# Seven products of quarters for three pairs of blocks in the second product of a transformer block

## The chip, the cores and the metric

The kernel runs on one core of one Trainium2 chip. Its time is device time in microseconds (us), from one launch. A core has TensorE (PE in the profile, its weight loads PEld), VectorE (DVE), ScalarE (ACT), GpSimd (POOL) and SyncE (SP, here a queue that issues transfers). Each takes its instructions in the order in which they are written, and semaphores hold one back until others are done.

## The reference

One block with 2048 tokens of width 512: local dilated attention, then a dense layer with a squared ReLU. The change lies in the last quarter of the dense layer.

```python
def _B_ref(x, w1, b1, w2, b2):          # x 2048x512, w1 512x1792, w2 1792x512
    h = jnp.einsum("bsd,df->bsf", x, w1) + b1
    r = jnp.where(h > zero, h, zero)
    h = r * r
    out = jnp.einsum("bsf,fd->bsd", h, w2) + b2
    return out

h = x + _A_ref(_layernorm(x, axis=-1), A_wqkv, A_wo)
h2 = h + _B_ref(_layernorm(h, axis=-1), B_w1, B_b1, B_w2, B_b2)
```

## The kernel before

Every float32 operand of a product is held as a high part (a cast, `hi`) and a low part (the difference, `lo`), and each product is three products of parts: high by high, low by high, high by low.

The tokens are worked on in four passages `u` of 512 tokens, four tiles of 128 each. The 1792 hidden units are 14 blocks `f` of 128. In a passage the *first product* (w1) makes a block of hidden values in a PSUM bank, ScalarE and VectorE turn it into the squared ReLU in two parts, and the *second product* (`mlp2`, w2) adds that block into four banks `acc`, one per tile: 12 matmuls of 512 columns (4 tiles, 3 terms). The high parts of w2 stay in `big_h`; the low parts of 12 blocks are stashed in DRAM (`w2l_d`), and some of them at a time lie in `big_l`, whence `fetch` brings the next when a place comes free. `big_l` also holds the transposed tokens.

In the last passage (`u` = 3) the first product goes by pairs of blocks (`PAIRS`, seven of them), each as seven products of quarters (Winograd's form of Strassen's scheme): a quarter has 256 features or 128 units or 256 tokens, so that each of the 7 products is 6 matmuls of 256 columns in place of 8 x 6 for the whole. It needs sums of quarters of the tokens (made once: `s32`, `a_h`, `a_l`) and of the weights, made for each pair: `t_load` brings the raw w1 columns (`traw`), `t_sums` makes four differences in place (on VectorE for pairs 0 and 1, on GpSimd after), `t_split` makes the parts `th` and `tl`. `products_a` does four products (24 matmuls) into the four banks `b` of the tuple `XB`, and copies two of them to `p`; `products_b` does the other three (18 matmuls), two of them on top of the first ones, and adds up. `second`, `squared` and `rest` make ReLU, square and parts of the pair's two blocks f and g (`r`, `rh`, `rl`).

No scheduler moves anything: an engine's order is the order of the code. `at(k, fn, ...)` puts a call off to the end of the k-th slot from now (`due`), and `end_slot` runs the calls of the current slot, so their place in an engine's order is the place of that `end_slot`. A step n of the last passage has two slots: `products_a(n)`, one second product; `products_b(n)`, another second product (from step 2 on). The raw weights of pair n + 2 are loaded at the start of step n, their sums made in its second slot, and their parts in the first slot of step n + 1. At the end, two blocks' second products go tile by tile, each tile followed by `finish` (the residual is added, the tile goes out), and `last_tile` does the last tile in two halves of 256 columns. Three things of earlier passages reach into this one: the residual `h` of the last tiles gets b2 on GpSimd (`add_b2`, L694), goes to DRAM (`spill`, L697), and comes back (`unspill`).

## Time and profile before

| | before |
|---|---|
| median of 3 runs (lowest to highest) | 501.11 us (500.86 to 548.89) |
| the profiled execution | 500.91 us |
| its span, first to last instruction | 499.1 us |
| TensorE busy, matmuls | 494.2 us (99%), 2411 |
| VectorE, ScalarE, GpSimd busy | 383.7, 305.7, 354.6 us |
| granted TensorE clock, mean | 1.000 of full speed |

The rows further down are of the profiled execution, in us from the start of its span. The time between the execution and its span, 500.91 - 499.1, lies around the kernel. In the rows of an engine a number in square brackets is its idle time before that instruction, with what ended it. Matmuls overlap, so the pace of a group is read from the chain, where each piece ends as the next begins.

### The profile page before, as it was taken

The numbers are of one execution on the slowest core, as the hardware profiler recorded it, in microseconds if no ns is written. First come the engines' busy times: TensorE is split into PE (matmuls) and PEld (weight loads), VectorE is DVE, ScalarE is ACT, GpSimd is POOL, SyncE is SP. The second block draws the span as 40 slices with busy tenths as digits, with TensorE's granted clock in tenths as the row PEclk, the third lists the DMA queues.
The fourth block names the chain that finished last, engine by engine and source line by source line (L and its number), as shares of the span: only waits on it lengthen the run. The fifth ranks groups of instructions, "written<-read, shape, count | busy, mean of one in ns | idle before, by whom it ended". The sixth has DMA issues, their size and how long they took to land.

```text
span 499.1 us, 7514 instructions
## 1 busy us (share of the span) xinstructions
PE 494.2 (99%) x2411; PEld 420.6 (84%) x2411; DVE 383.7 (77%) x526; ACT 305.7 (61%) x543; POOL 354.6 (71%) x429
## 2 busy tenths in 40 slices
PE   8999999999999999999999999999999999999997
PEld 7998888888888888888888888888888888998986
DVE  6479899999989989998979989897984257733233
ACT  4634778668346757478564556866454968766551
POOL 5714798996775999888878777787889353885610
PEclk9999999999999999999999999999999999999999
DMA  8779979889788899689776945977680575355212
GB/s 269 201 215 244 281 253 297 272 268 310 209 219 260 294 286 259 185 226 248 219 253 210 218 143 164 269 236 258 201 202 14 130 193 163 117 158 169 64 42 87
DMA packets 113584, 103.67 MB, mean 208 GB/s; under 512 B 33672, under 2 KB 82056, under 8 KB 113544
## 3 DMA queue, kind: packets, MB, share of 16 engines
q1 hardware_dynamic: 112600, 102.66, 70.1%
q10 hardware_dynamic: 944, 0.52, 0.3%
q8 instruction: 19, 0.31, 0.3%
q14 instruction: 21, 0.17, 0.1%
HBM read 72.65 MB, written 24.25 MB: 194 GB/s over the span
## 4 chain that ended last, share of the span: by engine, by line
PE 98%; DMA 1%; ACT 0%; ACTq 0%; DVE 0%; issue 0%
PE mm L231 49%; PE acc L924 30%; PE wo L231 9%; PE mm L837 7%; PE tr L204 2%; DMA wraw<-in_A_wqkv_dram 1%; PE half L947 0%; ACTq L570 0%; ACT big_h L152 0%; ACT xh L152 0%; DVE h L949 0%
## 5 line engine op out<-in xcount | busy, mean ns | idle before, releaser
L414 POOL TENSOR_TENSOR pr<-pr 128x512 f32<-128x512 f32 (+1 forms) x128 | 134.1, 1048 | 35.6 <-DVE pr L357 30.2
L231 PE MATMUL mm<-big_l,w_h 128*128 128x512 f32 x336 | 88.5, 390 | 0.0
L357 DVE TENSOR_TENSOR pr<-ex,v 128x1024 f32<-128x1024 f32 x62 | 75.6, 1221 | 12.0 <-POOL o L414 9.2
L344 DVE TENSOR_TENSOR pr<-qp,k 128x1024 f32<-128x1024 f32 x64 | 76.8, 1200 | 6.1 <-ACT qp L271 3.3
L380 DVE TENSOR_REDUCE ex<-pr 128x64 f32<-128x1024 f32 x64 | 78.4, 1225 | 1.8
L231 PEld LDWEIGHTS mm<-big_l,w_h 128*128 128x128 f32 x336 | 63.0, 188 | 13.4 <-ACT r L894 0.3
L155 POOL TENSOR_TENSOR rl<-r,rh 128x512 fp32r<-128x512 f32 x42 | 54.9, 1306 | 24.2 <-ACT rh L152 20.1
L231 PE MATMUL mm<-big_l,xh 128*128 128x512 f32 (+1 forms) x208 | 56.3, 379 | 0.0
L231 PE MATMUL mm<-big_h,xh 128*128 128x512 f32 (+1 forms) x208 | 53.1, 377 | 0.3 <-ACT xh L152 0.3
L231 PE MATMUL mm<-big_h,xl 128*128 128x512 f32 (+1 forms) x208 | 52.6, 374 | 0.0
L924 PE MATMUL acc<-big_h,rh 128*128 128x512 f32 x190 | 52.1, 391 | 0.0
L924 PE MATMUL acc<-big_l,rh 128*128 128x512 f32 x190 | 52.0, 390 | 0.0
L924 PE MATMUL acc<-big_h,rl 128*128 128x512 f32 x190 | 51.7, 390 | 0.0
L231 PE MATMUL mm<-big_l,w_l 128*128 128x512 f32 x168 | 44.9, 389 | 0.0
L231 PEld LDWEIGHTS mm<-big_h,xl 128*128 128x128 f32 x208 | 38.3, 188 | 6.0
L231 PEld LDWEIGHTS mm<-big_h,xh 128*128 128x128 f32 x208 | 37.9, 188 | 6.1 <-ACT xh L152 0.5
L924 PEld LDWEIGHTS acc<-big_h,rl 128*128 128x128 f32 x190 | 35.7, 188 | 7.4
L924 PEld LDWEIGHTS acc<-big_l,rh 128*128 128x128 f32 x190 | 35.6, 188 | 7.4
L231 PEld LDWEIGHTS mm<-big_l,xh 128*128 128x128 f32 x208 | 37.4, 188 | 4.9
L924 PEld LDWEIGHTS acc<-big_h,rh 128*128 128x128 f32 x190 | 35.1, 188 | 7.1 <-DVE h L932 0.3
L894 ACT ACTIVATE r<-mm,b_sb 128x512 f32<-128x512 f32 x42 | 28.7, 684 | 16.2 <-PE mm L231 15.7
L231 PEld LDWEIGHTS mm<-big_l,w_l 128*128 128x128 f32 x168 | 31.5, 188 | 6.6
(167 smaller groups left out, 919.4 us busy)
## 6 DMA issues: line engine op xcount, KB each, us to landing
k<-qkv_d SPq DMA_DIRECT2D x50, 288.0 KB, 3.2
v<-qkv_d SPq DMA_DIRECT2D x46, 288.0 KB, 3.2
qkv_d<-y SPq DMA_DIRECT2D x18, 512.0 KB, 4.0
big_l<-w2l_d SPq DMA_DIRECT2D x24, 256.0 KB, 3.1
xt<-in_A_x_dram SPq DMA_DIRECT2D x16, 256.0 KB, 4.2
q<-qkv_d SPq DMA_DIRECT2D x32, 128.0 KB, 3.6
h<-in_A_x_dram SPq DMA_DIRECT2D x16, 256.0 KB, 3.3
h_d<-h SPq DMA_DIRECT2D x16, 256.0 KB, 3.4
```

The lines of the kernel that those rows point to most:

```text
L155: eng.tensor_tensor(out=dst, in0=src, in1=h, op=ALU.subtract)
L204: nc.tensor.transpose(tr[:, k, :], src[:, k * P:(k + 1) * P], ident)
L231: nc.tensor.matmul(ps, l(k), r(k), start=(n == 0), stop=(n == 3 * KB - 1))
L344: nc.vector.tensor_tensor(out=pr.rearrange("p i w h d -> p i w (h d)"), in0=qps["now"][:, j % 2].unsqueeze(2).to_broadcast([P, RI, W, GC]) ...
L357: nc.vector.tensor_tensor(out=p2, in1=vwin, op=ALU.mult, in0=e1[:, :, :, j * GH:(j + 1) * GH].unsqueeze(4).to_broadcast([P, RI, W, GH, DH]))
L380: nc.vector.tensor_reduce(out=lf[:, :, :, j * GH:(j + 1) * GH], in_=pr, axis=X, op=ALU.add)
L414: nc.gpsimd.tensor_tensor(out=dst, in0=p2[:, :, :w], in1=p2[:, :, w:2 * w], op=ALU.add)
L837: nc.tensor.matmul(ps, sta[y][:, k], mov[x][:, k], start=(first and q == 0), stop=(last and q == len(terms) - 1), skip_group_check=True)
L894: nc.scalar.activation(r, ps, AF.Relu, bias=b1_sb[:, f:f + 1])
L924: nc.tensor.matmul(acc[j], l[:, j * P:(j + 1) * P], w[f], start=(first and n < len(js)), stop=(last and n >= len(terms) - len(js)))
```

## The change

The second product of the last three pairs, (0, 7), (1, 8) and (4, 11), is done by seven products of quarters as well. The four quarters of a product are now: 256 of the 512 tokens by one of the pair's two blocks for the hidden values, and one of the two blocks by 256 of the 512 output columns for w2. Each of the seven (`part`) is 6 matmuls of 256 columns, three terms by two tiles. What this needs: `v_load` brings the raw rows of w2 for a pair, `v_sums` makes four differences on GpSimd, `v_split` the parts; `s_sums` makes four sums of the pair's hidden quarters on VectorE (`x`), `s_split` their parts. Products 1, 5, 6 and 7 add up over the three pairs in the four banks `XB` (`outer`), 4, 3 and 2 go right into `acc` (`inner`, and the loop at the end); five sums (`v`, `u2`, `u3`, `s12`, `s22`) and eight half additions to `h` put them together. `last_tile` is gone; the last product of the last tile has a bank of its own (`z`).

The second product of the other eight blocks is as before, but `PLAN` gives each step one, after `products_a`; two are left for the end of the last step.

The hidden parts of the last passage are written into the columns of `w1_h` and `w1_l` that belong to their block and are no longer needed. The raw w1 columns are two tiles under the tags of the attention's k and v. `AHEAD` is a table of the steps' first and second slots: `t_load`, `t_sums` and `t_split` move a slot or a step forward, from pair 2 on; half of each `tl` now comes from VectorE (before: from pair 3 on, both halves from GpSimd). The four unspills come together after the last step.

```diff
+WN = 3
+PLAN = {n: (1, 0) for n in range(1, 7)}
+VS = {2: 0, 3: 1, 4: 2}
+VP = ()
 HOLD = 1.0
 XS = 6
...
     def t_load(n):
         f = PAIRS[n][0]
-        tw[n] = t_tile(n, "traw")
+        tw[n] = [att.tile([P, RI, 2, P], F32, name="traw", tag="kv"[n % 2]) for _ in range(2)]
         for k in range(KB):
-            nc.sync.dma_start(tw[n][:, k], bass.AP(
...
-        b11, b12, b21, b22 = [tw[n][:, 2 * k:2 * k + 2, c] for k in (0, 1) for c in (0, 1)]
+        b11, b12, b21, b22 = [t[:, :, c] for t in tw[n] for c in (0, 1)]
         tt, sub = (nc.vector if n < 2 else nc.gpsimd).tensor_tensor, ALU.subtract
         tt(out=b11, in0=b12, in1=b11, op=sub)
...
     def t_split(n):
-        h, l = t_tile(n, "th", F32R), t_tile(n, "tl", F32R)
-        hi(h, tw[n])
-        for k, eng in ((2, nc.vector if n < 3 else nc.gpsimd), (0, nc.gpsimd)):
-            lo(eng, l[:, k:k + 2], tw[n][:, k:k + 2], h[:, k:k + 2])
+        h, l = t_tile("th", "pr"), t_tile("tl", "o")
+        raw = tw[n]
+        for k in (1, 0):
+            hi(h[:, 2 * k:2 * k + 2], raw[k])
+        for k, eng in ((1, nc.vector), (0, nc.vector if n == 2 else nc.gpsimd)):
+            lo(eng, l[:, 2 * k:2 * k + 2], raw[k], h[:, 2 * k:2 * k + 2])
         tw[n] = h, l
...
         nc.scalar.activation(rf[:, :HD], b[1], AF.Relu, bias=b1_sb[:, f:f + 1])
         tt(out=u[:, HD:], in0=b[2], in1=p[:, :HD], op=ALU.add)
...
         nc.scalar.activation(r, r, AF.Square)
-        hi(rh, r)
-        lo(nc.vector, rl, r, rh)
-        hid[R - 1, f] = rh, rl
+        if f in PAIRS[-1]:
+            at(0, parted, f, r)
+        else:
+            parted(f, r)
+    def parted(f, r):
+        rh, rl = [w[:, :, f * P:(f + 1) * P] for w in (w1_h, w1_l)]
+        n = RI if f in WINO[:WN] else R
+        src = r.rearrange("p (j c) -> p j c", j=R)[:, :n]
+        hi(rh[:, :n], src)
+        lo(nc.vector, rl[:, :n], src, rh[:, :n])
...
+    PLAIN = len(PAIRS) - WN
+    WINO = [p[i] for i in range(2) for p in PAIRS[PLAIN:]]
+    whole, vw = {}, {}
+    def v_load(q):
+        vw[q] = row("vraw"), row("vraw")
+        for r, f in zip(vw[q], PAIRS[PLAIN + q]):
+            nc.sync.dma_start(r, w2[f * P:(f + 1) * P, :])
+    def v_sums(q):
+        (b11, b12), (b21, b22) = [(r[:, :HD], r[:, HD:]) for r in vw[q]]
+        tt, sub = (nc.vector if q in VP else nc.gpsimd).tensor_tensor, ALU.subtract
+        tt(out=b11, in0=b12, in1=b11, op=sub)
+        tt(out=b12, in0=b22, in1=b12, op=sub)
+        tt(out=b22, in0=b22, in1=b11, op=sub)
+        tt(out=b21, in0=b21, in1=b22, op=sub)
+    def v_split(q):
+        if q == 0:
+            t = [work.tile([P, D], F32R, name="rh", bufs=LAG + 1) for _ in range(4)]
+        else:
+            t = [a[:, i] for a in [att.tile([P, 2, D], F32R, name="vs", tag=tag, bufs=3)
+                                   for tag in ("pr", "o")] for i in range(2)]
+        raw = vw[q]
+        vw[q] = t[:2], t[2:]
+        for i in range(2):
+            hi(t[i], raw[i])
+            at(int(q < 2), lo, nc.gpsimd, t[2 + i], raw[i], t[i])
+    def s_sums(n):
+        rf, rg = whole.pop(n)
+        (a11, a21), (a12, a22) = [(r[:, :HD], r[:, HD:]) for r in (rf, rg)]
+        x = whole[n] = row("x"), row("x")
+        tt, sub = nc.vector.tensor_tensor, ALU.subtract
+        tt(out=x[0][:, :HD], in0=a21, in1=a22, op=ALU.add)
+        tt(out=x[1][:, :HD], in0=a11, in1=a21, op=sub)
+        tt(out=x[0][:, HD:], in0=x[0][:, :HD], in1=a11, op=sub)
+        tt(out=x[1][:, HD:], in0=a12, in1=x[0][:, HD:], op=sub)
+    def s_split(n):
+        for x, f in zip(whole.pop(n), PAIRS[n - PLAIN]):
+            src = x.rearrange("p (j c) -> p j c", j=R)
+            h, l = [w[:, :, f * P:(f + 1) * P] for w in (w1_h, w1_l)]
+            hi(h, src)
+            lo(nc.vector, l, src, h)
+    def part(n, m, ps, js, first=False, last=False):
+        q, (f, g) = n - PLAIN, PAIRS[n]
+        c, d = PAIRS[q]
+        col, i0 = {1: (f, 0), 2: (g, 0), 4: (g, 2), 5: (c, 0), 6: (c, 2), 7: (d, 0), 3: (d, 2)}[m]
+        sta = [w[:, :, col * P:(col + 1) * P] for w in (w1_h, w1_l)]
+        lo_, hi_ = slice(0, HD), slice(HD, D)
+        if m < 4:
+            w, cs = f if m == 1 else g, hi_ if m == 3 else lo_
+            mov = w2_h[w][:, cs], w2_l[w][:, cs]
+        else:
+            i, cs = {5: (0, lo_), 7: (0, hi_), 4: (1, lo_), 6: (1, hi_)}[m]
+            mov = [t[i][:, cs] for t in vw[q]]
+        terms = [(x, y, j) for x, y in ((0, 0), (1, 0), (0, 1)) for j in js]
+        for k, (x, y, j) in enumerate(terms):
+            nc.tensor.matmul(ps[j], sta[x][:, i0 + j], mov[y], start=first and k == 0,
+                             stop=last and k >= len(terms) - len(js), skip_group_check=True)
     def hidden(u, f, ps, wait=0):
...
+        at(wait, lo, nc.gpsimd, rl, r, rh)
+        hid[u, f] = [lambda j, a=a: a[:, j * P:(j + 1) * P] for a in (rh, rl)]
     def hidden_now():
...
+            nc.tensor.matmul(acc[j], l(j), w[f],
                              start=(first and n < len(js)),
...
+                             (15, at, 0, t_load, 2),
...
-    fs = [f for pair_ in PAIRS for f in pair_]
-    need = [f for f in fs if f < 12 and f not in place]
+    fs = [f for pair_ in PAIRS[:PLAIN] for f in pair_]
+    need = [f for f in fs + WINO if f < 12 and f not in place]
...
-    def second_product(last=False):
-        q = used[0]
-        f = fs[q]
-        if last:
-            mlp2(u, f, acc, js[:-1])
-            mlp2(u, f, acc, js[-1:], False, True)
-        else:
-            mlp2(u, f, acc, js, q == 0)
-        used[0] += 1
+    def refill(f):
         if f < 12 and need:
             free.append(place.pop(f))
             at(1, fetch, need.pop(0))
+    def second_product():
+        q = used[0]
+        mlp2(u, fs[q], acc, js, q == 0, q == len(fs) - 1)
+        used[0] += 1
+        refill(fs[q])
+    AHEAD = {"0a": ((t_split, 1),), "0b": ((t_load, 3), (t_sums, 2)),
+             "1a": ((t_split, 2), (t_sums, 3)), "1b": ((t_load, 4), (t_split, 3), (t_sums, 4)),
+             "2b": ((t_load, 5), (t_split, 4), (t_sums, 5)),
+             "3b": ((t_load, 6), (t_split, 5), (t_sums, 6)), "4b": ((v_sums, 0), (t_split, 6), (v_sums, 1)), "5b": ((v_sums, 2),)}
+    def ahead(step):
+        for fn, m in AHEAD.get(step, ()):
+            if fn is t_load:
+                fn(m)
+            else:
+                at(0, fn, m)
     for n in range(len(PAIRS)):
-        if n + 2 < len(PAIRS):
-            t_load(n + 2)
+        if n in VS:
+            v_load(VS[n])
         products_a(n)
         if not n:
-            at(0, t_split, 1)
+            ahead("0a")
             lo(nc.vector, a_l[4], s32[4], a_h[4])
         if n:
             at(0, second, n - 1)
-            if n + 1 < len(PAIRS):
-                at(0, t_split, n + 1)
-            second_product()
-        if n in (4, 5):
-            for i in range(2):
-                at(0, unspill, R * u + 2 * (n - 4) + i)
+            ahead(f"{n}a")
+            if n - 3 in VS and not VS[n - 3]:
+                at(0, v_split, 0)
+            if n == len(PAIRS) - 1:
+                at(0, s_split, n - 2)
+                at(0, v_split, 1)
+            for _ in range(PLAN[n][0]):
+                second_product()
         end_slot(5.6)
         products_b(n)
-        if n + 2 < len(PAIRS):
-            at(0, t_sums, n + 2)
-        if n > 1:
+        ahead(f"{n}b")
+        if n > PLAIN:
+            at(0, s_sums, n - 1)
+        for _ in range(PLAN[n][1] if n else 0):
             second_product()
         if n == len(PAIRS) - 1:
             at(0, second, n)
-            second_product(True)
+            at(0, s_sums, n)
+            at(0, s_split, n - 1)
+            at(0, at, 0, s_split, n)
+            at(0, at, 0, v_split, 2)
+            for i in js:
+                at(1, unspill, R * u + i)
+            while used[0] < len(fs):
+                second_product()
         end_slot(4.9)
-    h = hs[S // P - 1]
-    for j in js[:-1]:
-        for f in fs[-2:]:
-            mlp2(u, f, acc, [j], False, f == fs[-1])
-            if j == 0:
-                end_slot(0.65)
-        at(0, finish, R * u + j, acc[j])
-        if j == 1:
-            at(0, nc.vector.tensor_tensor, h, acc[-1], h, ALU.add)
-        if j:
-            run(due)
-    last_tile(S // P - 1, fs[-2:])
+    two = {m: psum.tile([P, D], F32, name="part", tag=tag) for m, tag in zip((1, 5, 6, 7), XB)}
+    halves = {m: [t[:, j * HD:(j + 1) * HD] for j in range(RI)] for m, t in two.items()}
+    both, left, right = range(RI), slice(0, HD), slice(HD, D)
+    head, end = PLAIN, len(PAIRS) - 1
+    def outer(n):
+        for m in (1, 6, 5, 7) if n < end else (1, 6, 7, 5):
+            part(n, m, halves[m], both, n == head, n == end)
+        refill(PAIRS[n][0])
+        run(due)
+        now["slot"] += 1
+    def inner(n, m):
+        part(n, m, [acc[RI + j][:, left] for j in both], both, False, n == end)
+    for n in range(head, end):
+        outer(n)
+    inner(head, 4)
+    outer(end)
+    tt = nc.vector.tensor_tensor
+    v, u2, u3, s12, s22 = [row("c") for _ in range(5)]
+    nc.scalar.copy(v, two[1])
+    tt(out=u2, in0=two[6], in1=v, op=ALU.add)
+    tt(out=u3, in0=two[7], in1=u2, op=ALU.add)
+    tt(out=s22, in0=two[5], in1=u3, op=ALU.add)
+    tt(out=s12, in0=two[5], in1=u2, op=ALU.add)
+    for eng, i, cs, src in ((nc.gpsimd, 0, left, v), (nc.gpsimd, 1, left, v),
+                            (nc.gpsimd, 2, left, u3), (nc.gpsimd, 3, left, u3),
+                            (nc.vector, 2, right, s22), (nc.vector, 3, right, s22),
+                            (nc.gpsimd, 0, right, s12), (nc.gpsimd, 1, right, s12)):
+        h = hs[R * u + i][:, cs]
+        eng.tensor_tensor(out=h, in0=h, in1=src[:, i % RI * HD:(i % RI + 1) * HD], op=ALU.add)
+    for n in range(head + 1, end + 1):
+        inner(n, 4)
+    for i in (2, 3):
+        finish(R * u + i, acc[i])
+    z = psum.tile([P, D], F32, name="part", tag=XB[0])[:, left]
+    for m, j, ps in ((3, 0, acc[0][:, right]), (2, 0, acc[0][:, left]),
+                     (3, 1, acc[1][:, right]), (2, 1, z)):
+        for n in range(head, end + 1):
+            part(n, m, [ps, ps], [j], ps is z and n == head, n == end)
+        if m == 2 and not j:
+            finish(R * u, acc[0])
+    h = hs.pop(R * u + 1)
+    b, e = divmod(u, 2)
+    tt(out=h, in0=acc[1], in1=h, op=ALU.add)
+    nc.scalar.dma_start(out_v[b, e, 1, :, right], h[:, right])
+    tt(out=h[:, left], in0=z, in1=h[:, left], op=ALU.add)
+    nc.sync.dma_start(out_v[b, e, 1, :, left], h[:, left])
```

TensorE at the end of the last step, from the last product of `products_b` of pair 6 on (`mm`: bank of a first product, `acc`: bank of a tile, `big_h`: high parts of w2, `big_l`: low parts; `rh`, `rl` or `w_h`, `w_l`: the hidden parts). Before:

```order
L837 MATMUL mm<-wo_l,w_h 128x256 x2
L924 MATMUL acc<-big_h,rh 128x512 x4
L924 MATMUL acc<-big_l,rh 128x512 x4
L924 MATMUL acc<-big_h,rl 128x512 x4
L924 MATMUL acc<-big_h,rh 128x512 x3
L924 MATMUL acc<-big_l,rh 128x512 x3
L924 MATMUL acc<-big_h,rl 128x512 x3
```

TensorE at the same place now (`part`: one of the four banks of the new products; `rh` here: parts of the w2 sums):

```order
L843 MATMUL mm<-wo_l,w_h 128x256 x2
L1006 MATMUL acc<-big_h,w_h 128x512 x4
L1006 MATMUL acc<-big_l,w_h 128x512 x4
L1006 MATMUL acc<-big_h,w_l 128x512 x4
L1006 MATMUL acc<-w_x,w_h 128x512 x8
L1006 MATMUL acc<-w_x,w_l 128x512 x4
L970 MATMUL part<-big_h,w_h 128x256 x2
L970 MATMUL part<-big_h,w_l 128x256 x2
L970 MATMUL part<-big_l,w_h 128x256 x2
L970 MATMUL part<-rh,w_h 128x256 x2
```

Two whole second products stand behind the last step, and then the new products of 256 columns, where blocks of the last pairs went tile by tile.

GpSimd in steps 1 and 2, from the bias of tile 14 on (`h`: residual, `traw_4642`: raw columns of pair 2, `traw_4734`: of pair 3, `r`: the sum of L869). Before:

```order
L694 TENSOR_TENSOR h_4278<-h_4278,b2_sb_81 128x512
L155 TENSOR_TENSOR tl_4791<-traw_4642,th_4790 128x512
L694 TENSOR_TENSOR h_4341<-h_4341,b2_sb_81 128x512
L869 TENSOR_TENSOR r_4816<-u_4744,p_4743 128x256
L805 TENSOR_TENSOR traw_4734<-traw_4734 128x2x128
```

GpSimd at the same place now (`traw_4719`, `traw_4720`: pair 3; `traw_4829`: pair 4; L877 is what L869 was):

```order
L698 TENSOR_TENSOR h_4278<-h_4278,b2_sb_81 128x512
L809 TENSOR_TENSOR traw_4719<-traw_4719 128x2x128
L810 TENSOR_TENSOR traw_4719<-traw_4720,traw_4719 128x2x128
L811 TENSOR_TENSOR traw_4720<-traw_4720,traw_4719 128x2x128
L812 TENSOR_TENSOR traw_4720<-traw_4720 128x2x128
L698 TENSOR_TENSOR h_4341<-h_4341,b2_sb_81 128x512
L877 TENSOR_TENSOR r_4823<-u_4748,p_4747 128x256
L159 TENSOR_TENSOR tl_4841<-traw_4719,th_4840 128x512
L809 TENSOR_TENSOR traw_4829<-traw_4829 128x2x128
```

The four differences of pair 3 stand ahead of the second bias addition and of the sum of L877.

ScalarE from `products_b` of step 2 into step 3 (`th_4889`: pair 3; `r_4912` and `r_4913`: the two blocks of pair 2; `p_4951`: the copies of step 3's banks). Before:

```order
L152 CAST th_4889<-traw_4734 128x1024
L866 ACTIVATE r_4912<-mm_4838,b1_sb_83 128x256
L873 ACTIVATE r_4912<-r_4912,b1_sb_83 128x256
L884 ACTIVATE r_4912<-r_4912 128x512
L152 CAST rh_4933<-r_4912 128x512
L850 COPY p_4951<-mm_4947 128x256
L856 COPY p_4951<-mm_4950 128x256
L879 ACTIVATE r_4913<-r_4913,b1_sb_83 128x512
```

ScalarE at the same place now (`th_4939`: pair 4; `r_4921`, `r_4922`: pair 2; `p_4957`: step 3's copies):

```order
L874 ACTIVATE r_4921<-mm_4854,b1_sb_83 128x256
L881 ACTIVATE r_4921<-r_4921,b1_sb_83 128x256
L891 ACTIVATE r_4921<-r_4921 128x512
L156 CAST w1_h_88<-r_4921 128x4x128
L156 CAST th_4939<-traw_4830 128x512
L156 CAST th_4939<-traw_4829 128x512
L856 COPY p_4957<-mm_4953 128x256
L862 COPY p_4957<-mm_4956 128x256
L887 ACTIVATE r_4922<-r_4922,b1_sb_83 128x512
```

The cast of the weights' sums, now in halves and for one pair further on, stands ahead of the two copies of the next step's banks.

## Rows read from the trace of the kernel before

**Rows 1.** The page, part 1: busy us (share of the span) and instructions.

```profile
PE 494.2 (99%) x2411; PEld 420.6 (84%) x2411; DVE 383.7 (77%) x526; ACT 305.7 (61%) x543; POOL 354.6 (71%) x429
```

**Rows 2.** The chain that ended last, merged: start, us, engine, line, count.

```profile
422.05 7.92 PE mm L837 x66
429.96 2.97 PE acc L924 x12
...
445.61 2.87 PE mm L837 x24
448.49 2.75 PE acc L924 x12
...
482.79 2.15 PE mm L837 x18
484.94 9.55 PE acc L924 x42
494.49 1.44 PE half L947 x12
...
495.96 0.42 DVE h L949
```

**Rows 3.** Waits from 400 us on, by total: us, times, longest.

```profile
PEld acc L924 <- DVE h L932: 0.3, 1, 0.3
```

**Rows 4.** ScalarE's timeline in steps 3 and 4: start, us, line, operation.

```profile
450.24 1.05 ACT L152 CAST th<-traw 128x1024 fp32r<-128x1024 f32 x1
451.98 0.47 ACT L866 ACTIVATE r<-mm,b_sb 128x256 f32<-128x256 f32 x1 [0.69 <-PE mm L837]
453.62 0.51 ACT L873 ACTIVATE r<-r,b_sb 128x256 f32<-128x256 f32 x1 [1.16 <-DVE r L868]
454.16 0.63 ACT L884 ACTIVATE r<-r 128x512 f32<-128x512 f32 x1
454.82 0.62 ACT L152 CAST rh<-r 128x512 fp32r<-128x512 f32 x1
456.88 0.37 ACT L850 COPY p<-mm 128x256 f32<-128x256 f32 x1 [1.44 <-PE mm L837]
...
458.59 0.73 ACT L879 ACTIVATE r<-r,b_sb 128x512 f32<-128x512 f32 x1
```

**Rows 5.** GpSimd's timeline, steps 0 to 3: L869, sums, bias, lows.

```profile
428.11 0.74 POOL L869 TENSOR_TENSOR r<-u,p 128x256 f32<-128x256 f32 x1
428.81 0.75 POOL L805 TENSOR_TENSOR traw<-traw 128x256 f32<-128x256 f32 x1
...
432.48 1.75 POOL L694 TENSOR_TENSOR h<-h,b_sb 128x512 f32<-128x512 f32 x1
...
435.90 1.29 POOL L694 TENSOR_TENSOR h<-h,b_sb 128x512 f32<-128x512 f32 x1
...
447.01 0.74 POOL L805 TENSOR_TENSOR traw<-traw 128x256 f32<-128x256 f32 x1
...
449.47 0.74 POOL L808 TENSOR_TENSOR traw<-traw 128x256 f32<-128x256 f32 x1
451.37 2.55 POOL L155 TENSOR_TENSOR tl<-traw,th 128x512 fp32r<-128x512 f32 x2 [1.16 <-ACT th L152]
```

**Rows 6.** SyncE's issues in step 2: the spill of tile 15, raw columns.

```profile
437.30 0.54 SPq L697 DMA_DIRECT2D h_d<-h  x1
...
438.42 2.51 SPq L798 DMA_DIRECT2D traw<-in_B_w_dram  x4
```

**Rows 7.** Transfers from 400 us on: count, size, median us to landing.

```profile
traw<-in_B_w_dram SPq DMA_DIRECT2D x26, 128.0 KB, 2.8
```

**Rows 8.** VectorE's timeline: the same low part, steps 3 and 5.

```profile
455.48 1.20 DVE L155 TENSOR_TENSOR rl<-r,rh 128x512 fp32r<-128x512 f32 x1 [1.56 <-ACT rh L152]
...
476.52 0.69 DVE L155 TENSOR_TENSOR rl<-r,rh 128x512 fp32r<-128x512 f32 x1 [1.56 <-ACT rh L152]
```

**Rows 9.** The page, part 5: weight loads of the second product, mean ns.

```profile
L924 PEld LDWEIGHTS acc<-big_h,rl 128*128 128x128 f32 x190 | 35.7, 188 | 7.4
```

More of the change, by code (lines that the diff above doesn't have):

```diff
@@ L882, in squared @@
     def squared(f, r):
-        rh, rl = work.tile([P, D], F32R, name="rh", bufs=LAG + 1), row("rl", dt=F32R)
         nc.scalar.activation(r, r, AF.Square)
-        hi(rh, r)
-        lo(nc.vector, rl, r, rh)
-        hid[R - 1, f] = rh, rl
-    hid = {}
+        if f in PAIRS[-1]:
[8 more added lines that the diff above has]
+        lo(nc.vector, rl[:, :n], src, rh[:, :n])
+        hid[R - 1, f] = [lambda j, a=a: a[:, j] for a in (rh, rl)]
@@ L896, in hidden @@
         hi(rh, r)
-        at(wait, lo, nc.vector if u == R - 1 else nc.gpsimd, rl, r, rh)
-        hid[u, f] = rh, rl
+        at(wait, lo, nc.gpsimd, rl, r, rh)
+        hid[u, f] = [lambda j, a=a: a[:, j * P:(j + 1) * P] for a in (rh, rl)]
     def hidden_now():
@@ L923, in mlp2 @@
                 mid()
-            nc.tensor.matmul(acc[j], l[:, j * P:(j + 1) * P], w[f],
+            nc.tensor.matmul(acc[j], l(j), w[f],
                              start=(first and n < len(js)),
```

20 lines of the change are left out of this document (5 added, 15 removed).

## The prediction, made before the change was run

> **What bounds the kernel now.** I read the page's busy line first, then the chain of work that ended last, then the waits, then each engine's timeline in the last passage. TensorE is busy 99% of the span, every other engine 77% or less [rows 1]. From 422.05 to 495.93 us the chain holds nothing but matmuls, L837 and L924 by turns and L947 at the end [rows 2], and after 400 us the only wait that TensorE has is 0.3 us, for a bank that L932 reads [rows 3]; it lies in the product at 429.96, which takes 2.97 us where its like takes 2.75 [rows 2]. So the passage costs what its matmuls cost, and an engine beside TensorE matters only where its lateness reaches TensorE's next bank or operand. What is left after the last matmul is one addition (0.42 us at 495.96) and an output transfer, up to 499.1.
>
> **Matmuls removed and added.** The six blocks of the last three pairs now take 66 matmuls of 512 columns and 12 of 256. Of these, 42 are the 9.55 us group and 12 the 1.44 us group; the other 24 run at 2.75 us per 12, 5.50 us [rows 2]. Together 16.49 us. The change puts in 7 products x 3 pairs x 6 matmuls = 126 of 256 columns. The rows have this shape in L837: 2.87 us for 24 and 2.15 for 18, 0.1195 us each [rows 2]; 126 x 0.1195 = 15.06 us (15.12 at L947's 0.120). The gain is 1.43 us (1.37 with the other rate). The columns fall by 12.5% and the time by 8.7% only, since two matmuls of 256 columns cost 0.239 us and one of 512 costs 0.229. All other matmuls of the passage (294 of L837, 96 of L924) stay. TensorE would then end near 494.5 us, if nothing makes it wait.
>
> The Trainium skill, "TensorE: Matmul & The Clock Gate", section "Back-to-back issue gap", gives a sustained 131 ns for a matmul of 512 columns and 81 ns for one of 128. An estimate from that page for 256 columns, halfway between on a straight line in N, is some 98 ns, and by it the change would lose 2.5 us, 126 x 0.098 against 66 x 0.131 + 12 x 0.098. This trace disagrees, with 229 ns and 119.5 ns [rows 2]; the sum goes by the trace.
>
> **The cover that goes.** Before, a step of the passage was a (2.87), a second product (2.75), b (2.15) and another second product (2.75), 10.52 us. Now the second one comes only after the last step, so steps 2 to 6 are 7.77 us, with b of one pair right before a of the next. The same work of the other engines, and more, has to fit there.
>
> ScalarE per step: two casts of th of 512 each (0.62 as the cast in the rows; before one of 1024 at 1.05), L866 0.47, L873 0.51, L884 0.63 and cast 0.62, two copies of 0.37, then L879 0.73, L884 0.63 and cast 0.62 [rows 4]: 6.19 us of 7.77. What counts is the order in its queue. After b ends (448.49 + 2.75 + 2.15 = 453.39) L873 starts at 453.62, 0.23 later. From there 0.54, 0.66 and 0.62 bring the cast's end to 2.05 us after b; the casts of th, now in front of the copies, to 3.3; the copies to 4.05; L879, L884 and the cast to 6.0. The next b's first product ends 2.87 + 2.75 + 0.72 = 6.34 after the last b, so L866 is free to start at about 6.54 and ends at 7.0; the next a needs its bank at 7.77. The copy of bank 1 is done at 3.7 and b adds into that bank from 5.62. So no wait: the room is 0.77 us at bank 1 of a and 1.9 us at bank 1 of b. VectorE has the other banks ready in time too: of b, only bank 3 ends at b's end, and a writes it 1.43 us later. It is likewise free in step 1 of the kernel before, where two groups a and b already run without a product between (422.05, 66 matmuls in 7.92 us, 0.12 each, [rows 2]).
>
> **The sums moved ahead.** GpSimd's queue changes most. A full set of four sums takes 3.67 us from 428.81 to the bias at 432.48, and 3.20 from 447.01; a bias addition 1.75 and 1.29; a half of tl 1.28 (two in 2.55) [rows 5]. Per step it has L869 0.74, one half of tl 1.28 and a set of sums 3.20: 5.2 of 7.77 us. The tight place is once, in steps 1 to 3. There GpSimd does, after L869 from 428.11, the sums of pair 2, the bias of tile 14, the sums of pair 3 and the bias of tile 15, one after the other: 428.85 + 3.20 + 1.29 + 3.20 + 1.29 = 437.8 at the quick rows, 439.7 at the slow ones (before: 437.19). SyncE's queue holds the spill of tile 15 behind that bias, and the load of pair 4 behind the spill: 0.11 to the issue, 0.64 for it, 1.88 up to the last of four issues [rows 6], 2.8 us to landing [rows 7], 5.4 us in all. Raw weights are there at 443.2 or 445.1; three sums more (2.4, or 2.9 in the slow set) give 445.6 or 448.0; two casts of th 446.9 or 449.2; and behind them in ScalarE's queue the copy of bank 1, 447.2 or 449.6. TensorE wants b of pair 3 at 448.45 (422.05 + 5.02 + 2.87 + 2.97 + 2.15 + 2.87 + 2.75 + 2.15 + 2.87 + 2.75). So it has 1.2 us of room, or waits 1.2. Behind the copy, ScalarE's 0.37 + 0.73 + 0.63 + 0.62 + 0.47 put the end of L866 at 450.1 or 452.4, where a of pair 4 is due at 450.6 or, 1.2 later, 451.8: another 0.6 us in the slow case, 1.8 in all. The same queue of GpSimd holds L869 of pair 1 behind the bias of tile 15, and ScalarE's L879 behind that: with 0.74 + 0.73 + 0.63 + 0.62 + 0.47 the L866 of pair 2 ends at 442.9 even at the slow rows, where a of pair 3 is due at 442.83. So this term lies between 0 and 1.8 us. The rows beside it in time are mixed (3.67 and 1.75, then 1.29), and I take 0.5, nearer to the quick ones, because only the first set and the first bias there were slow.
>
> **The new operands.** Six loads of w2 rows go on SyncE between those of w1, of the size of the stashed halves that it already brings; nobody needs them for two steps. Their sums and lows come on GpSimd from step 4: L869, two sets of sums and a half of tl are 0.74 + 3.20 + 1.28 + 3.20 = 8.4 us, then L869, two lows and a set 6.5, then L869 and four lows 5.9. In 21 us from 458.4 (the end of b of pair 4) that is 479.3. ScalarE's end sets the last lows rather: after the last b it has about 1 us of lateness from four extra casts in step 6, then L873, L884, L879, L884 (2.8) and some seven and a half casts (4.75), then one low of 1.28 and another: 10.5 us after b. The product that reads them comes 5.5 + 2.87 + 2.87 + 0.72 + 0.72 = 12.7 after b. Room 2.2 us, no wait. The last products need stashed halves of blocks 7, 8 and 11, which are fetched behind the four unspills, at least 6 us ahead.
>
> **The tail.** v, u2, u3, s22 and s12 and eight half additions lie beside the 1.43 + 4.3 us of matmuls that follow the last product 5: s12 is there 1.6 us after it, GpSimd's last two additions (0.74 each) at 3.2, and the last two additions of VectorE wait for matmuls only. After the last matmul stand 0.42 and a half tile's transfer, as now: 0, within 0.3 either way.
>
> **Sum.** The profiled execution took 500.91 us (span 499.1), 0.20 below the median of the runs shown, whose undisturbed ones are 500.86 and 501.11; I forecast on its scale. 500.91 - 1.43 + 0.5 = 499.98, so **500.0 us**.
>
> **Rivals.** *GpSimd late (ends slower):* every operation of it as slow as the slow rows. For it: VectorE has more two-input operations in a step, and its low takes 1.20 us at 455.48, beside GpSimd's sums, and 0.69 alone at 476.52 [rows 8]. Against: in the passage GpSimd's sums come back to 3.20. It costs 1.8 us at pair 4 and gives 500.91 - 1.43 + 1.8 = 501.3; a second such wait at a later pair, of the same 1.2, gives 502.5. It turns the gain into a loss when the sums of pair 4 end after about 447.6 us. The Trainium skill, "SBUF — State Buffer", section "Who interferes with whom", says that a VectorE instruction with two inputs in SBUF contends with a GpSimd one that reads SBUF, one blocking the other; the trace agrees (1.20 against 0.69), and by that rule alone the longer rows would be the usual ones, 501.3. *ScalarE late in every step:* its 6.0 us chain grows by over 1.3 us, each of four steps loses the rest, say 1 us: 503.5. Against: 1.3 us is a fifth of the chain. *Narrow matmuls held up by their weight loads:* a load takes 188 ns [rows 9], and if it no longer lay beside the matmul before it, 126 x 0.188 = 23.7 us in place of 16.49 would give 508.1. Against: 294 matmuls of L837 load weights of the same size and run at 0.1195. The page on TensorE named above points the same way, with its estimate of 2.5 us lost. *A longer tail*, by 1 us, because an addition on GpSimd is late: 501.0.
>
> **Chances.** Forecast (499.2 to 500.9, wait 0 to 1.4) 0.62; GpSimd late (500.9 to 502.5) 0.22; ScalarE late 0.06; tail 0.04; narrow matmuls 0.01; else 0.05. The range runs from no wait with a tail 0.3 shorter, 499.2, to the far end of the first rival, 502.5. Two per cent, 10 us, is about what a measurement of this kernel can tell from no change; none of these cases reaches it, so within 2% has 0.97, slower 0.02 for a stall that I do not see, faster 0.01.
>
> **What would show it.** Right: the chain from 422 us still all TensorE, 126 matmuls in about 15.1 us, steps of 7.77, waits of TensorE below 1.4 us, all at pairs 3 and 4 on ScalarE's copy or L866's bank. Wrong: waits at every a (ScalarE), a gap before the last outer products (lows late), matmuls above 0.12 us, or over 3.3 us between the last matmul and the end.

## The result, and the profile after

The changed kernel takes 502.23 us (median of 9 runs, 502.05 to 502.62), the kernel before 500.89 (9 runs). One run of the kernel before was slow, 548.89 us, and is left out of the ratio. The ratio is 1.0028 with a 95% interval of 1.0017 to 1.0039. That is within 2% and inside the range, but on the other side of the kernel before than forecast: 1.3 us slower, where 0.9 faster was predicted. The profiled execution took 502.23 us with a span of 500.2 (before 500.91 and 499.1). In the new code L861 and L875 are the additions of `u` that were L855 and L867, L874 is what L866 was, L877 what L869 was, L159 the low parts (L155).

The page, part 1, after (busy us, share of the span, instructions; [rows 1] before):

```profile
PE 493.5 (99%) x2459; PEld 421.9 (84%) x2459; DVE 404.2 (81%) x554; ACT 311.8 (62%) x563; POOL 373.3 (75%) x448
```

TensorE is busy 0.7 us less, as its matmuls cost less, and yet the span is 1.1 longer. The chain that ended last, after, from 422 us (start, us, engine, line, count; [rows 2] before):

```profile
422.17 2.89 PE mm L843 x24
...
434.41 1.22 DVE tl L159
435.63 0.35 DVE u L875
436.02 2.49 PE mm L843 x18
...
449.04 5.52 PE mm L843 x42
...
457.30 5.03 PE mm L843 x42
...
469.67 0.88 DVE x L944
470.55 1.44 DVE x L945
471.99 1.45 DVE x L946
...
474.23 0.42 DVE u L861
...
474.69 1.70 PE mm L843 x12
476.39 5.47 PE acc L1006 x24
481.86 5.75 PE part L970 x48
...
495.89 1.09 PE part L970 x9
```

Read it from below. The 126 new matmuls stand without a gap from 481.86 to 496.98: 15.12 us (15.06 forecast). But the chain is no longer TensorE alone. Twice it goes over to VectorE: to the low parts of pair 2 ahead of L875, and to the hidden sums of pair 4 (L944 to L947) ahead of L861. A third delay stands inside a TensorE row: 42 matmuls in 5.52 us where their like take 5.03. The waits of TensorE from 422 us on, after (us, times, longest; [rows 3] before):

```profile
PEld mm L843 <- DVE u L861: 1.3, 1, 1.3
PEld mm L843 <- DVE u L875: 0.5, 1, 0.5
PEld mm L843 <- ACT r L874: 0.2, 1, 0.2
```

Of 2.0 us of waits, 1.8 are on VectorE's additions, and 0.2 (the delay inside the 5.52 us row) on the chain of GpSimd, SyncE and ScalarE that I had priced. Two rows of VectorE's timeline show what stood ahead of L875 in step 1, the next five what stood ahead of L861 in step 6, and the last two the same sums again, two sets later (start, us, operation):

```profile
432.92 2.71 DVE L159 TENSOR_TENSOR tl<-traw,th 128x512 fp32r<-128x512 f32 x2
435.55 0.41 DVE L875 TENSOR_TENSOR u<-mm,p 128x256 f32<-128x256 f32 x1
...
469.60 0.95 DVE L944 TENSOR_TENSOR x<-r 128x256 f32<-128x256 f32 x1
470.47 1.52 DVE L945 TENSOR_TENSOR x<-r 128x256 f32<-128x256 f32 x1
471.92 1.52 DVE L946 TENSOR_TENSOR x<-x,r 128x256 f32<-128x256 f32 x1
473.47 0.84 DVE L947 TENSOR_TENSOR x<-r,x 128x256 f32<-128x256 f32 x1
474.23 0.41 DVE L861 TENSOR_TENSOR u<-mm,p 128x256 f32<-128x256 f32 x1
...
482.89 0.42 DVE L945 TENSOR_TENSOR x<-r 128x256 f32<-128x256 f32 x1
483.23 0.42 DVE L946 TENSOR_TENSOR x<-x,r 128x256 f32<-128x256 f32 x1
```

The set that ran from 469.60 to 474.3 takes 4.7 us; at the rows from 482.9 on it would take 1.7. What differs is GpSimd, whose timeline after has the following (its last row, two lows of the last pair's w2, is used again under "The new operands"):

```profile
437.81 1.30 POOL L698 TENSOR_TENSOR h<-h,b_sb 128x512 f32<-128x512 f32 x1
...
470.23 2.92 POOL L159 TENSOR_TENSOR rh<-vraw,rh 128x512 fp32r<-128x512 f32 x2
...
478.91 2.99 POOL L159 TENSOR_TENSOR vs<-vraw,vs 128x512 fp32r<-128x512 f32 x2
485.82 3.28 POOL L159 TENSOR_TENSOR vs<-vraw,vs 128x512 fp32r<-128x512 f32 x2 [3.92 <-ACT vs L156]
```

Its two lows lie over L945 and L946 from 470.2 to 473.1; from 482 to 485.8 it is idle. The set of sums that VectorE makes from 478.9 on stands beside two more lows, and its L945 and L946 take 1.52 and 1.51 us again. The bias of tile 15 ends at 439.1, where I had 437.8 to 439.7 from [rows 5]: GpSimd is slowed too, towards its slow rows.

A wait also costs more than its own length. TensorE's timeline around the longest one (x2: two matmuls in one row):

```profile
473.17 0.40 PE L843 MATMUL mm<-big_l,w_h 128*128 128x256 f32 x2
474.69 0.50 PE L843 MATMUL mm<-wo_h,th 128*128 128x256 f32 x2 [1.12 <-DVE u L861]
475.03 0.40 PE L843 MATMUL mm<-wo_h,tl 128*128 128x256 f32 x2
```

The first pair behind the wait takes 0.50 us where others take 0.40; behind the other two waits a second step of 0.08 follows. I therefore added up, over all matmuls of the passage, how much later than usual each starts (usual: 0.120 us behind one of 256 columns, 0.227 behind one of 512). This **loss** is 0.22 us before and 2.56 after. The matmuls save 1.37, the loss costs 2.34 more, the passage begins 0.12 later, the tail is 0.05 longer and 0.22 more lies outside the span: 500.91 - 1.37 + 2.34 + 0.39 = 502.27, measured 502.23.

### The profile page after: what moved, and what is told of

Read it like the earlier page. It is cut to its first block, busy times and chain, and to the rows that moved or that the text cites. A ratio compares the mean times of both kernels' runs of the same rounds, so it can differ in the third digit from the quotient of the medians.

```text
span 500.2 us, 7714 instructions
## 1 busy us (share of the span) xinstructions
PE 493.5 (99%) x2459; PEld 421.9 (84%) x2459; DVE 404.2 (81%) x554; ACT 311.8 (62%) x563; POOL 373.3 (75%) x448
## 4 chain that ended last, share of the span: by engine, by line
PE 94%; DVE 2%; DMA 1%; POOL 1%; ACT 1%; issue 1%; ACTq 0%; POOLq 0%
PE mm L235 49%; PE acc L1006 26%; PE wo L235 9%; PE mm L843 5%; PE tr L208 2%; PE part L970 2%; PE acc L970 1%; DMA wraw<-in_A_wqkv_dram 1%; DVE tl L159 0%; DVE x L946 0%; DVE x L945 0%; ACT th L156 0%; POOL traw L811 0%; DVE u L875 0%; DVE x L944 0%
## 5 line engine op out<-in xcount | busy, mean ns | idle before, releaser
L159 POOL TENSOR_TENSOR rl<-r,rh 128x512 fp32r<-128x512 f32 x42 | 54.4, 1295 | 24.3 <-ACT rh L156 19.9
L1006 PE MATMUL acc<-big_l,rh 128*128 128x512 f32 x144 | 38.8, 390 | 0.0
L1006 PE MATMUL acc<-big_h,rl 128*128 128x512 f32 x144 | 38.5, 389 | 0.0
L1006 PE MATMUL acc<-big_h,rh 128*128 128x512 f32 x144 | 38.5, 389 | 0.0
L540 ACT COPY y<-mm 128x512 f32<-128x512 f32 x36 | 21.1, 585 | 23.3 <-PE mm L235 19.1
L418 POOL TENSOR_TENSOR o<-pr 128x128 f32<-128x128 f32 x64 | 31.5, 491 | 5.0
L407 ACT ACTIVATE ex<-ex 128x256 f32<-128x256 f32 (+1 forms) x20 | 6.5, 327 | 41.4 <-DVE ex L403 41.3
```

The lines of the kernel that those rows point to most:

```text
L159: eng.tensor_tensor(out=dst, in0=src, in1=h, op=ALU.subtract)
L418: nc.gpsimd.tensor_tensor(out=dst, in0=p2[:, :, :w], in1=p2[:, :, w:2 * w], op=ALU.add)
L540: nc.scalar.copy(dst, src)
L1006: nc.tensor.matmul(acc[j], l(j), w[f], start=(first and n < len(js)), stop=(last and n >= len(terms) - len(js)))
```

## Experiments

The theory: GpSimd's and VectorE's work with two operands in SBUF hold each other up, and the time is lost where one of VectorE's bank additions stands behind such work. The main rival: the lateness comes by the chain that I had priced (GpSimd's sums, SyncE's spill, ScalarE's L874). Each kernel's median, ratio with interval to the kernel before run beside it, and loss as defined above, which is that of its one profiled execution:

| kernel | us | ratio to before | loss, us |
|---|---|---|---|
| changed kernel | 502.23 | 1.0028 [1.0017, 1.0039] | 2.56 |
| 1 sums behind L861 | 502.54 | 1.0027 [1.0017, 1.0037] | 2.87 |
| 2 GpSimd idle there | 500.98 | 0.9999 [0.9990, 1.0009] | 0.92 |
| 3 low of pair 2 on GpSimd | 503.86 | 1.0053 [1.0036, 1.0070] | 4.21 |
| 4 second part alone | 501.28 | 1.0004 [0.9994, 1.0013] | 0.66 |
| 5 first part alone | 503.90 | 1.0063 [1.0050, 1.0075] | 4.08 |
| 6 low behind L875 | 502.95 | 1.0045 [1.0032, 1.0059] | 3.07 |
| 7 last transfers exchanged | 502.35 | 1.0033 [1.0021, 1.0046] | 2.81 |
| 8 second weights on VectorE | 501.70 | 1.0018 [1.0009, 1.0027] | 2.30 |
| 9 and the bias later | 502.39 | 1.0028 [1.0018, 1.0038] | 3.09 |
| 10 bias later, without 8 | 504.22 | 1.0063 [1.0051, 1.0076] | 3.92 |
| 11 bias on VectorE | 500.32 | 0.9985 [0.9976, 0.9994] | 0.60 |
| 12 bias behind L861 | 499.78 | 0.9970 [0.9959, 0.9982] | 0.10 |

Line numbers shift by up to ten in these kernels; the text keeps those of the changed kernel.

**1. The hidden sums of pair 4 behind L861.**

```diff
         products_a(n)
+        if n == len(PAIRS) - 1:
+            s_sums(n - 2)
...
-        if n > PLAIN:
+        if n > PLAIN + 1:
             at(0, s_sums, n - 1)
```

> The four hidden sums of pair 4 stand behind L861 of step 6 on VectorE instead of ahead of it. Theory (VectorE's sums, held up by GpSimd, make L861 late and TensorE waits 1.3 us for its bank in b of step 6): that wait is gone. The sums themselves stay long (4.7 us against 1.7 alone), since GpSimd works beside them. But the lows of the last pair's w2 sums were ready at 489.1 us, 0.4 us before TensorE reads them, so up to 0.9 us of the gain comes back as a wait in the last outer product: 501.0 to 501.8 against 502.2 of the changed kernel. Rival (the wait is for something else that VectorE needs, such as ScalarE's copy of bank 1): the wait in b stays, 502.2.

The wait in b of step 6 is gone, and others took its place further on; the time is the same, above the range of the theory. Waits of TensorE, this kernel:

```profile
PEld part L970 <- DVE w_l L159: 0.7, 1, 0.7
...
PEld part L970 <- POOL vs L159: 0.5, 1, 0.5
```

The sums are as long as before (0.63, 1.52, 1.51 and 0.84 us) at their new place, so work behind them is late: the lows of pair 5's sums, and GpSimd's lows of the second weights, for which I had forecast 2.2 us of room. Order alone does not help while the operations stay long.

**2. GpSimd idle beside the hidden sums.** The two lows of the first pair's w2 sums are left out, the high parts being read in their place, and so are the four differences of the last pair.

```diff
-"4b": ((v_sums, 0), (t_split, 6), (v_sums, 1)), "5b": ((v_sums, 2),)}
+"4b": ((v_sums, 0), (t_split, 6), (v_sums, 1))}
...
-        vw[q] = t[:2], t[2:]
+        vw[q] = t[:2], t[2:] if q else t
...
-            at(int(q < 2), lo, nc.gpsimd, t[2 + i], raw[i], t[i])
+            if q:
+                at(int(q < 2), lo, nc.gpsimd, t[2 + i], raw[i], t[i])
```

> Leaves out part of the computation: the two lows of the first pair's w2 sums (its high parts are used in their place) and the four w2 differences of the last pair, so that GpSimd has nothing to do while VectorE makes the hidden sums of pair 4 ahead of L861. Order on VectorE unchanged. Theory (GpSimd's operations hold VectorE's up): L944 to L947 of pair 4 take 0.42 us each, some 1.7 us together instead of 4.7, the 1.3 us wait in b of step 6 is gone, 500.9 or less. Rival (these operations are that long by themselves, by their operands): L945 and L946 stay at 1.5 us, the wait stays, 502.2.

VectorE's timeline, this kernel, the same four sums (L945 to L948 here) and L861:

```profile
469.78 0.96 DVE L945 TENSOR_TENSOR x<-r 128x256 f32<-128x256 f32 x1
470.67 0.41 DVE L946 TENSOR_TENSOR x<-r 128x256 f32<-128x256 f32 x1
471.00 0.41 DVE L947 TENSOR_TENSOR x<-x,r 128x256 f32<-128x256 f32 x1
471.45 0.42 DVE L948 TENSOR_TENSOR x<-r,x 128x256 f32<-128x256 f32 x1
471.79 0.42 DVE L861 TENSOR_TENSOR u<-mm,p 128x256 f32<-128x256 f32 x1
```

With GpSimd idle, the two sums that took 1.52 us take 0.41, the wait is gone, and the kernel is 1.25 us quicker. This is the test of the theory: VectorE's own instructions and their order are the same.

**3. The second half of pair 2's low on GpSimd**, to take the wait of 0.5 at 436 us away.

```diff
-        for k, eng in ((1, nc.vector), (0, nc.vector if n == 2 else nc.gpsimd)):
+        for k, eng in ((1, nc.vector), (0, nc.gpsimd)):
```

> The second half of pair 2's weight lows goes from VectorE to GpSimd, as for later pairs. Theory: the 0.48 us wait in a of step 2, behind two lows of 2.7 us on VectorE, goes; but GpSimd's queue gets 1.3 to 1.75 us ahead of the sums of pair 3 and the bias of tile 15, so the load of pair 4 and the casts of its sums come that much later, and the waits at pairs 3 and 4 (0.24 us now) grow by 1.3 to 2.2 us: 503.0 to 504.0. Rival (that chain has more room than worked out): 501.7.

It went, and the chain that I had priced came in its place. Waits of TensorE, this kernel:

```profile
PEld mm L843 <- ACT r L874: 1.6, 2, 1.2
...
PEld mm L843 <- ACT p L856: 1.1, 2, 0.6
```

So that chain is real; in the changed kernel it is only 0.2 us late.

**4. The second part of the change alone**: the kernel before, with the new `AHEAD` table without `v_sums` and the two lows of pair 2 on VectorE.

```diff
+    AHEAD = {"0a": ((t_split, 1),), "0b": ((t_load, 3), (t_sums, 2)),
...
-        if n + 2 < len(PAIRS):
-            t_load(n + 2)
```

> The kernel before with the second part of the change alone: the first weights' loads, differences and parts by the table, two tiles of raw columns, two casts, half of each low part on VectorE; the second product stays whole, two in each step. Theory (this part costs only where VectorE's two lows of pair 2 make L875 of step 1 late, 0.5 us; from step 2 on a step is 10.5 us): 500.9 to 501.4, with a wait of TensorE of at most 0.5 us in a of step 2. Rival (moving the weights' sums ahead is itself what costs): over 501.8, with waits in later steps.

One wait of 0.5 us (for L875's counterpart), 0.4 us more lost than before: working further ahead costs that and brings nothing by itself. The medians do not tell the two kernels apart (0.9994 to 1.0013).

**5. The first part alone**: the new products, with the old distance of the first weights. The second half of pair 2's low is on GpSimd here too, as in kernel 3.

```diff
+    AHEAD = {f"{n}a": ((t_split, n + 1),) for n in range(6)}
+    AHEAD.update({f"{n}b": ((t_sums, n + 2),) for n in range(5)})
...
+        if n + 2 < len(PAIRS):
+            t_load(n + 2)
         products_a(n)
```

> The first part of the change alone: the seven products, with the differences of the first weights at the distance of the kernel before (loaded two steps ahead, summed after b, split after the next a). Theory (the losses are where a bank's addition stands on VectorE behind two-input work that GpSimd draws out): the wait of 0.48 at step 2 falls away, the one of 1.3 in b of step 6 stays; steps of 7.77 leave room for the casts and lows of the weights, which end some 7.3 us after the last b where a product reads them at 8.5; 501.3 to 501.7. Rival (the step further ahead is needed, since a step without its second product in the middle is too short): a wait of 0.5 to 1.3 in each of four steps, 503 to 506.

My theory fell here. Waits of TensorE, this kernel:

```profile
PEld mm L843 <- ACT r L874: 2.1, 2, 1.1
PEld mm L843 <- POOL tl L159: 1.8, 1, 1.8
```

L874 is 1.0 us late twice. In step 2 it stands in ScalarE's queue behind casts of pair 3, whose sums GpSimd ended at 441.7 after waiting twice for their load (0.40 and 0.56 us); in step 5 behind a cast of w2 differences that GpSimd ended at 466.7. The third wait is for a low of pair 6, behind both sets of w2 differences on GpSimd. GpSimd sat idle for 0.40 us between its low of pair 2 and the sums of pair 3, so that low is not what made them late there, though no run has the old distance with that low on VectorE. With the second part of the change the first is 1.7 us quicker: it makes the room on GpSimd and ScalarE that the w2 work then takes.

**6. The second half of pair 2's low behind L875.**

```diff
+        lo(nc.vector, l[:, 2:], raw[1], h[:, 2:])
+        if n == 2:
+            at(1, lo, nc.vector, l[:, :2], raw[0], h[:, :2])
```

> The changed kernel with one move on VectorE: the second half of pair 2's low part behind the bank additions of step 1 in place of ahead of them. Theory: the wait of 0.48 at the a of step 2 falls away and nothing takes its place, since the product that reads that half comes 3.6 us after the bank is wanted; 501.75 (501.6 to 501.9). Rival (the bank is late for another reason, or the low is read too late and GpSimd's and ScalarE's queues shift): the wait comes back elsewhere, 502.2.

The wait at 436 us went, and 0.5 us came at 443 on ScalarE's L874 (total 0.9, where it was 0.2). It comes from GpSimd: L877 of pair 1 starts only at 439.4, behind the sums of pair 3 and the bias of tile 15, and ScalarE's activation waits 1.17 us for it. The earlier wait had covered this one: TensorE had come 0.5 us later.

**7. The last two transfers exchanged between SyncE's and ScalarE's queues.**

```diff
-    nc.scalar.dma_start(out_v[b, e, 1, :, right], h[:, right])
+    nc.sync.dma_start(out_v[b, e, 1, :, right], h[:, right])
...
-    nc.sync.dma_start(out_v[b, e, 1, :, left], h[:, left])
+    nc.scalar.dma_start(out_v[b, e, 1, :, left], h[:, left])
```

> The changed kernel with the last two transfers exchanged between the queues of SyncE and ScalarE, so that ScalarE's queue has the last half tile, as in the kernel before. The four profiled runs with the new products have 2.03 to 2.13 us outside the span, the two with the old second product 1.80 and 1.81. If the queue that issues last makes that difference, 1.8 outside and 502.0; if it does not (the rival), 2.05 outside and 502.2 as before.

1.99 us outside the span, and 2.01 on average over its runs as over those of the changed kernel: no effect. These averages are 1.95 to 2.36 us in the kernels with the new products, 1.79 to 1.82 in the two without; I did not find why. The loss is 2.81 here and 2.56 in the changed kernel, though nothing ahead of the last transfers differs (the delay near 451 us is 0.8 in place of 0.5): the losses of single executions are to be read with some 0.3 either way.

**8. The second weights on VectorE**, with moves 1 and 6, and the second set of their differences one slot later.

```diff
-VP = ()
+VP = (0, 1, 2)
...
-            at(int(q < 2), lo, nc.gpsimd, t[2 + i], raw[i], t[i])
+            at(int(q < 2), lo, nc.vector, t[2 + i], raw[i], t[i])
```

> The changed kernel with all differences and low parts of the second weights on VectorE in place of GpSimd, the hidden sums of pair 4 behind the addition that frees bank 2 in step 6, and the second half of pair 2's low behind the bank additions of step 1. Theory (the two engines hold each other up, and VectorE does this work in 0.42 and 0.69 us where it is alone): TensorE waits 0.3 us or less after 422 us, 500.4 (500.2 to 500.8), below both kernels. Rival (VectorE is too full: 9.2 us more of it between 455 and 489 us): new waits of 0.5 to 1.5 us for bank additions in steps 5 and 6 or for the lows of the hidden sums, 501 to 502.

From 470 us on TensorE waits no more, though VectorE has 9 us of work added: the hidden sums are at 0.42 again, and the last lows of the second weights end at 486.1, where they ended at 489.1 on GpSimd (the new products start at 481.1 and 481.7). Left are the waits of kernel 6 in steps 2 to 4, and 0.4 for one L875 behind a set of w2 differences: 501.7, in the rival's range though VectorE was not too full.

**9. The bias of tile 15 and its spill one place later**, and two of the w2 sets later on VectorE.

```diff
-2 + 3 * a + b + (t == 15), 3 + 3 * a + b + (t == 15))
+2 + 3 * a + b + 2 * (t == 15), 3 + 3 * a + b + 2 * (t == 15))
```

> The version before it with two moves more: the bias of tile 15 and its spill one place later (behind the sum that b of step 1 leaves to GpSimd, so that the load of pair 4 no longer stands behind the spill), and the last two sets of differences of the second weights one place later on VectorE, behind the additions that free bank 2 in steps 5 and 6. Theory: what was left of the waits, 1.4 us and some 0.2 us behind each of them, stood behind these two; TensorE waits 0.2 us or less and the kernel takes 499.8 (499.4 to 500.2), 1.1 below the kernel before. Rival (the next engine is late as soon as this one is not, as in the two runs that took one wait away): waits of 0.7 us or more in steps 2 to 4, 500.6 or more.

The losses up to 455 us fell to 0.1, and then TensorE stood for 1.7 us at 456; waits of 0.3 and 0.4 follow. The spill waits in SyncE's queue for the bias, which GpSimd now has behind the sums of pair 4. SyncE's timeline, this kernel: the fetch ahead of the spill, the spill, the w2 rows and the load of pair 5:

```profile
437.67 0.55 SPq L1188 DMA_DIRECT2D big_l<-w2l_d  x1
445.38 0.33 SPq L701 DMA_DIRECT2D h_d<-h  x1
445.76 2.10 SPq L920 DMA_DIRECT2D vraw<-in_B_w_dram  x2
447.96 2.51 SPq L802 DMA_DIRECT2D traw<-in_B_w_dram  x4
```

Seven microseconds without an issue; the load of pair 5 comes 4.2 us later than in the changed kernel (443.78 there). I had counted what the spill stood ahead of at its old place, not at the new one.

**10. The same bias with the second weights on GpSimd**: the changed kernel with the diffs of kernels 6 and 9 (bias and spill) alone.

> The changed kernel with the second half of pair 2's low behind the bank additions of step 1, and the bias of tile 15 and its spill one place later; the second weights stay on GpSimd. Theory: of the losses of TensorE in the changed kernel the ones at 436 and 451 us go (1.1 us with what follows each wait), the one at 474 stays (1.4); 501.1 (500.9 to 501.4). Rival (the bias is not what made ScalarE late in steps 2 and 3): 502 or more, as without that move.

The same stop at 456 us (1.1), and 1.9 us for L861 in step 6: it tells the two halves apart no further, since the fault of kernel 9 is in it.

**11. Kernel 9 with that bias on VectorE.**

```diff
-        nc.gpsimd.tensor_tensor(out=h, in0=h, in1=b2_sb, op=ALU.add)
+        eng = nc.vector if t == 15 else nc.gpsimd
+        eng.tensor_tensor(out=h, in0=h, in1=b2_sb, op=ALU.add)
```

> The version before it, with the bias of tile 15 on VectorE in place of GpSimd, at the same later place, so that its spill leaves SyncE's queue before the loads of the second weights and of pair 5 (the version before it held them behind the spill for 7 us). Theory: all waits seen in these runs are one order of four queues; with this one gone TensorE loses 0.4 us or less after 422 us (waits and what follows each) and the kernel takes 499.9 (499.6 to 500.3), 1.0 below the kernel before. Rival (each move only brings up the next queue): over 1 us lost at another place, 500.6 or more.

One wait of 0.4 us is left, for L861 of step 2 behind that bias (1.78 us beside GpSimd's sums).

**12. The bias behind that addition.**

```diff
+        if n == 2:
+            add_b2(15)
+            spill(15)
```

> The version before it with one move: the bias of tile 15 on VectorE right behind the addition that frees bank 2 in step 2, where it stood ahead of it. Theory: the one wait left after 422 us (0.40 us and 0.10 behind it, at 441.2) goes; TensorE loses some 0.1 us there and the kernel takes 499.8 (499.5 to 500.1), 1.0 below the kernel before. Rival (the bias, 1.78 us there beside GpSimd's sums, only moves the wait to the next bank addition of step 2): 500.3 or more, as before the move.

No wait is left after 400 us. The chain of this kernel from step 3 on is TensorE alone, in steps of 7.78 us:

```profile
448.80 5.03 PE mm L847 x42
453.84 2.75 PE acc L1010 x12
456.58 5.03 PE mm L847 x42
```

The ratio is 0.9970 (0.9959 to 0.9982), some 1.5 us below the kernel before that ran beside it, and its median is 2.4 below that of the changed kernel. Over all kernels with the new products, median less loss lies between 499.3 and 500.3, nine of twelve within 0.3 of 499.7; for the two with the old ones (before, and kernel 4) it is 500.7 and 500.6. So the products are worth about 1.0 us, and the rest of the differences is loss.

## Why the prediction was wrong

**Matmuls removed and added: right.** 126 in 15.12 us, 0.120 each. The gain of 1.37 to 1.43 is there in every run with the new products. The straight line drawn between the figures of the Trainium skill, "TensorE: Matmul & The Clock Gate", section "Back-to-back issue gap", would have had the new products lose; 256 columns are a third of the way on that line, not halfway, but the 98 ns that I gave are its value there, and the trace has 120.

**The cover that goes: the step that failed.** I wrote that "VectorE has the other banks ready in time too" and supported it by bank 3 of b and by step 1 of the kernel before. I walked ScalarE's queue row by row, and VectorE's not at all, though the change put two lows of pair 2 ahead of L875 and a set of hidden sums ahead of L861, in step 1, where a follows b at once as it did before, and in step 6, where the second product between a and b covers 2.75 us, and the sums took 4.7. So VectorE's lateness stood at nothing in the sum, and it measured 0.66 us at 436 and 1.38 at 474, slow starts included: 2.04 of the loss of 2.56. None of the signs of being wrong that I listed is a wait for VectorE. In step 1 it is the lows and not the missing cover, since kernel 4, which takes no cover away, has the same wait. Kernel 2 shows why the sums are long, kernels 8 (from 470 us on) and 12 that the waits end when VectorE meets no such work.

**The sums moved ahead: right in kind, and not what counted.** The chain of GpSimd, SyncE and ScalarE was priced at 0 to 1.8 us of waits and taken at 0.5. It came at pair 4, where I had put it: 0.24 us in two waits, for L874 and for the L875 right behind it, and 0.28 in slow starts, so 0.52 in this execution. Kernels 3 and 6 show single waits of 1.2 and 0.5 for it as soon as GpSimd gets more work, or TensorE comes earlier.

**The sum.** The term for waits, 0.5 with 1.8 as its far end, measured 2.34: a loss of 2.56 (2.0 in waits, 0.6 in slow starts behind them, which I had not counted) less the 0.22 of before. Another 0.4 came from the start of the passage, the tail and the time outside the span (0.22 of it), which I had put at nothing.

**The new operands.** The last low ends at 489.1, and is read at 489.4: 0.3 us of room where I had 2.2. The terms that I wrote down add up to 11.1 us after the last b, not 10.5, so the room should have read 1.6; the two lows then began 0.9 later than that sum has them, behind ScalarE's casts, and took 3.28 us in place of 2.56. In kernel 1 the same place became a wait of 0.5.

**The rivals.** *GpSimd late* gave 501.3 to 502.5 and the result lies there, with slow rows as the cause, as I wrote; its place, the sums of pair 4, is not where most of the time went, so that the range holds the result is luck. I took the low of 1.20 us in [rows 8] as a warning for GpSimd, when it was a row of VectorE. The Trainium skill, "SBUF — State Buffer", section "Who interferes with whom", says that a VectorE instruction with two SBUF inputs contends with a GpSimd one that reads SBUF, and that one with at most one SBUF input, outside the two-port modes, does not. The runs agree with both halves (below), and I should have given that rule more than 0.22. *ScalarE late in every step*, *narrow matmuls* and *a longer tail* did not come; a weaker form of the first is what kernel 5 has.

What stays open: why 0.15 to 0.56 us more lie outside the span with the new products (kernel 7 excludes the last queue); what each of kernel 12's moves is worth alone, since a wait taken away lets the next one show; and the lows ahead of L875 in step 1, of which the rows show that two take 2.71 us beside GpSimd's bias and sums, and no run has GpSimd idle there.

## What to carry to other kernels

When a change takes cover from TensorE, walk every engine's queue up to each bank that TensorE writes next, VectorE's first, and use the durations beside a busy neighbour (here 1.52 us for 0.42), not the quickest rows. A wait that is removed alone may give nothing, because it covers the next: kernels 1, 3 and 6 each removed one and none became faster, where the moves of kernel 12 together gave 2.4 us. An operation that feeds a transfer is moved together with all that is queued behind that transfer (kernel 9).
